# Rounded matmuls that walk their 512 columns as 64 lines of 8, in four passes

## The chip, the cores and the metric

The kernel runs on one core of one Trainium2 chip. The metric is the device time of one execution in microseconds (us), as the median of a few runs. Most executions of one kernel agree within 0.3%.

## The reference

The reference is an attention over a set, then a two-layer network. For each of four batches of 12,480 tokens with 128 features, 32 inducing vectors attend to the tokens, which gives 32 vectors `h`; then every token attends to these 32 vectors. The result, 49,920 tokens of 128 features, goes through the network.

```python
def mab(q, kv):
    s = scale * (q @ kv.transpose(0, 2, 1))
    s = s - s.max(-1, keepdims=True)
    a = np.exp(s)
    a /= a.sum(-1, keepdims=True) + 1e-09
    return a @ kv
h = mab(I, x)
x = mab(x, h)                       # 49,920 x 128
h = x @ w_in                        # 128 x 2048
g = h * (1.0 / (1.0 + np.exp(-1.702 * h)))
out = g @ w_out                     # 2048 x 128
```

## The kernel before

The tokens go through the network in blocks of 512, four blocks to a group of 2,048. A batch has six such groups (`s` = 0 to 5) and a rest of 192 tokens (`s` = 6); the rests of two batches together make one block of 384. The 2,048 hidden features are cut into 16 chunks of 128, and two chunks (`NG` = 8 pairs for a block) are one step `i` of the main loop (L1516).

The attention's weights are never multiplied with `h` by themselves. The kernel forms `hw` = `h` times `w_in` once for a batch, so that the hidden layer of a block is one product of `hw` with the block's attention weights. Both are stored in 32-row parts for the rounded value and what was left over by rounding, stacked to 128 rows: `st` (512 columns, of dtype `F32R`, a 4-byte float rounded for TensorE) is the stack of a block, `left` is that of a block of rests.

- `hidden` (L1368) issues for each of the two chunks one matmul: `hw` is the stationary operand (128x128), `st` the moving one (512 columns), and the output is half of a PSUM tile `ph` of two banks. For a block of rests it issues two of 192 columns for a chunk.
- `first` (L1382) calls `hidden`, and lets ScalarE apply the activation to `ph` (1,024 columns in one instruction) into `g`. Then ScalarE or VectorE writes `hi`, which is `g` rounded to `F32R`, and VectorE writes `lo` = `g` - `hi`.
- `second` (L1397) adds one chunk to the output: three matmuls with 128x128 weights, `hi` with the low part `wl` of `w_out`, `lo` with its high part `wh`, and `hi` with `wh`. All 48 of a block accumulate in one PSUM bank, `pso`. After the last, ScalarE copies the bank to `ob`, and a DMA stores it.

The first eight steps (`WHOLE` = 8) are done otherwise: `hidden` is the same, but their second layer is a product in plain float32 (`pso<-g,whole`), one matmul for a chunk.

The order of all engines' instructions is written out by a planner at build time. It keeps a clock for each engine, and costs (L277 for TensorE) that depend on the number of elements of an operand (`width`, L238) and on its dtype. `Clocks.names` (L87) tells which 512-column parts of some tiles an operand touches, from its first and last element. Beside the main loop run the attentions of the next batches, put between its steps. Their matmuls have 32 output rows (`128*32` in the profile) and run four side by side, one on each quarter of the array's columns.

Some of these walk their moving operand in lines already: `first_products` (L487) of batch 0, for the groups `s` whose tokens are not loaded a second time in rows (0, 3, 4 and 5: the list `LOADS` has `n6`, `n2` and `n1` alone), takes 16 lines of 32 columns, each fourth line of `xt`. Groups 2 and 1 take 512 columns in a row. By the order of `LOADS`, the groups' products come in the order 4, 3, 0, 5, 5 again (`TWICE`), 2, 1. `more_weights` (L1186) does the same with 12 of the 16 lines. The output of every matmul of this kernel is written to columns that lie side by side.

```python
xg = xg.rearrange("c (k g i) -> c g k i", g=g, i=32)      # first_products, batch 0
for j in range(g):
    pe_.matmul(pa[32 * j:32 * j + 32, 0:w], indT_sb, xg[:, j], start=True, stop=True)
```

Of the kernel before, what the change touches and what calls it, by code (L numbers as in the profile page):

```python
# [20 lines left out]
P = 128  # L21
# [42 lines left out]
S2 = ((6, 0), (1, 2, 3), (4, 5))  # L64
S2_LATER = ((0, 6), (1, 2, 3), (4, 5))
FB = 6
WINDOW = 100.0
CHAIN = 200.0
CALM = 0
# [4 lines left out]
class Clocks:  # L74
# [12 lines left out]
    def names(self, ap):  # L87
        name = ap.tensor.name
        if name not in self.halved:
            return [name]  # L90
        per = max(1, ap.ap[0][0] // (WC * len(self.halved[name])))
        at = ap.offset % ap.ap[0][0]
        end = (at + sum(step * (n - 1) for step, n in ap.ap[1:])) // per
        at //= per
        return self.halved[name][at // WC:end // WC + 1]
# [103 lines left out]
class Jobs:  # L199
# [13 lines left out]
    def step(self, limit=None, but=None):  # L213
        able = []
        for job in self.threads:
            eng, tiles, when = job[1]
            if eng is but or when is not None and not when():
                continue
            t = max(eng.t, self.clocks.ready(*(tiles() if callable(tiles) else tiles)))
            if limit is None or t <= limit(eng):  # L220
                able.append((t, job))
        if not able:
            return False
        soonest, job = min(able, key=lambda x: x[0])
        eng = job[1][0]
        t, job = min(
            [x for x in able if x[1][1][0] is eng and x[0] <= soonest + (CHAIN if x[1][2] <= -20 else WINDOW)],
            key=lambda x: (x[1][2], x[0]),
        )
        if self.idle:  # L230
            self.idle(t)
        job[1] = next(job[0], None)
        if job[1] is None:
            self.threads.remove(job)
        return True


def width(ap):  # L238
# [4 lines left out]
def set_attention_then_moe(ctx: ExitStack, tc, xT, x, indT, w_in, w_out, outT):  # L243
# [50 lines left out]
    pe_ = Meter(clocks, nc.tensor, tensor_cost, 220)  # L294
# [66 lines left out]
    hw = {}  # L361
# [514 lines left out]
    def start(pf, pw):  # L876
# [11 lines left out]
        for what in LOADS.split():  # L888
# [5 lines left out]
            elif what[0] == "n":  # L894
                if s < NS - 1:
                    t = pf.tile([P, BLK, P], F32, tag="xf", name="xf", bufs=FB)
                else:
# [114 lines left out]
        def turning(s, k0):  # L1012

            yield pe_, [xts[0, s]], bank("ph")
            if k0 == 0:
                turned[s] = pf.tile([P, BLK, P], F32, tag="xf", name="xf", bufs=FB)
            src = xts[0, s].rearrange("c (k t) -> c k t", t=P)
# [326 lines left out]
    def undivided(i):  # L1344

        yield pe_, lambda: [stacks[0, 0, 0], hw[0, i // 2]], bank(
            "ph", ("stack", 0), ("hw", i // 2), ("first", i - 1), ("second", i - AHEAD)
        )
        ph = hidden(i)
        hold("ph")  # L1350
        done.add(("first", i))
        yield act, [ph], has("exps")
        g = ph_.tile([P, 2, TOK], F32, tag="hi", name="g")
        act.activation(g, ph, AF.Gelu_apprx_sigmoid)
        hold("ph", -1)
        parts[i] = g, g
        done.add(("g", i))

    def undivided_seconds():

        while under_way:
            i, c = under_way[0]
            what = ("w_out", (2 * i + c) // 4)
            yield pe_, lambda: [parts[i][0], whole[(2 * i + c) // 4]], has(("g", i), what, *[("ahead", s) for s in AHEAD_S])
            second(*under_way.pop(0))
            done.add(("second", i))

    def hidden(i):  # L1368
        bi, k = divmod(i, NG)
        key, of = work[bi]  # L1370
        st = stacks[key]
        ph = ps_h.tile([P, 2, 512], F32, tag="ph", name="ph")
        for c in range(2):
            ch = 2 * k + c
            for b, at, w, _ in of:
                pe_.matmul(
                    ph[:, c, at:at + w], hw[b, ch // 4][:, ch % 4 * P:(ch % 4 + 1) * P],
                    st[:, at:at + w], start=True, stop=True,
                )
        return ph  # L1380

    def first(i):  # L1382
        ph = hidden(i)
        n = sum(p[2] for p in work[i // NG][1])
        hi = ph_.tile([P, 2, TOK], F32R, tag="hi", name="hi")
        lo = ph_.tile([P, 2, TOK], F32R, tag="lo", name="lo")
        g = pg.tile([P, 2, TOK], F32, tag="g", name="g")
        ph, hi, lo, g = ph[:, :, 0:n], hi[:, :, 0:n], lo[:, :, 0:n], g[:, :, 0:n]
        act.activation(g, ph, AF.Gelu_apprx_sigmoid)
        if act.t + 165 + 1.667 * n <= max(dve.t, act.t) + 150 + 1.06 * n:  # L1390
            act.activation(hi, ph, AF.Gelu_apprx_sigmoid)
        else:
            dve.tensor_copy(hi, g)
        dve.tensor_sub(lo, g, hi.bitcast(F32))
        parts[i] = hi, lo

    def second(i, c):  # L1397
        bi, k = divmod(i, NG)
        key, of = work[bi]
        n = sum(p[2] for p in of)  # L1400
        ch = 2 * k + c
        if ch == 0:
            outs[bi] = ps_o.tile([P, 512], F32, tag=f"po{bi % 2}", name="pso")
        o = outs[bi][:, 0:n]
        hi, lo = parts.pop(i) if c else parts[i]
        last = ch == NCH - 1
        if i < WHOLE:
            pe_.matmul(
                o, whole[ch // 4][:, ch % 4 * P:(ch % 4 + 1) * P], hi[:, c, :],
                start=(ch == 0), stop=last,  # L1410
            )
            if i >= WHOLE - NG and ch % 4 == 3:
                done.add(("whole", ch // 4))
        else:
            wlc, whc = [x[ch // 4][:, ch % 4] for x in (wl, wh)]
            pe_.matmul(o, wlc, hi[:, c, :], start=(ch == 0), stop=False)
            pe_.matmul(o, whc, lo[:, c, :], start=False, stop=False)
            pe_.matmul(o, whc, hi[:, c, :], start=False, stop=last)
        if last:
            ob = po.tile([P, TOK], F32, tag="ob", name="ob")  # L1420
            if bi == len(work) - 1:
                for k, (b, at, w, t0) in enumerate(of):
                    if k % 2:
                        dve.tensor_copy(ob[:, at:at + w], o[:, at:at + w])
                        nc.scalar.dma_start(outT[:, t0:t0 + w], ob[:, at:at + w])
                    else:
                        act.copy(ob[:, at:at + w], o[:, at:at + w])
                        sp.dma_start(outT[:, t0:t0 + w], ob[:, at:at + w])
                return
            act.copy(ob[:, 0:n], o)  # L1430
            for b, at, w, t0 in of:
                stores.append((i + 3, outT[:, t0:t0 + w], ob[:, at:at + w]))
            outs.pop(bi)
# [38 lines left out]
    n = len(work) * NG  # L1472
# [42 lines left out]
    i = WHOLE  # L1515
    while i < n or under_way:  # L1516
# [3 lines left out]
        if not begin_group(i):  # L1520
            at, c = under_way.pop(0)
            while not decoded(at, c):
                jobs.step(but=pe_)
            second(at, c)
        else:
            if back is None and turns and i >= begin[turns[0]] - LAST * (turns[0] not in es):
                back, laid = lay_out()
            while back is not None and first_block[laid] * NG <= i:
                late[0] = True
                run(back)  # L1530
                late[0] = False
                back = None
                if turns and first_block[turns[0]] * NG <= i:
                    back, laid = lay_out()
            bi, k = divmod(i, NG)
            while work[bi][0] not in stacks or any((p[0], k // 2) not in hw for p in work[bi][1]):
                jobs.step()
            while used["ph"] and jobs.step(but=pe_):
                pass
            while any(("two", q) not in done for q in range(min(G, (i + 4) // NG + 1))):  # L1540
                jobs.step(but=pe_)
            first(i)
            under_way += [(i, 0), (i, 1)]
            i += 1
            next(rest, None)
            if back is not None and next(back, 0) == 0:
                back = None
# [35 lines left out]
```

## Time and profile before

| | |
|---|---|
| median of 3 runs | 1539.06 us (1538.87 to 1539.07) |
| span of the profiled execution, first to last instruction | 1537.2 us (no time of its own is listed for it; the median of the runs is 1.9 us above its span) |
| TensorE matmul (PE) busy | 1529.9 us, 7736 instructions |
| TensorE weight load (PEld) busy | 1229.4 us |
| VectorE (DVE) busy | 1301.1 us |
| ScalarE (ACT) busy | 1345.4 us |
| mean granted TensorE clock | 1.000 |

Nearly every instruction has the line L181, because the planner's helper issues it; groups are told apart by their tiles. Matmuls are pipelined: each lasts longer than the distance between the starts of two neighbours, so the busy time of a group of matmuls is not their count times their duration. What a matmul costs the engine is the distance from its start to the next one's. The ends of matmuls are modelled.

### The profile page before, as it was taken

The page shows a single profiled execution, that of the slowest core. Times are in us where ns is not written, and L with a number is a line of the kernel's source. Part 1 is how long each engine was busy: PE and PEld are TensorE (multiplying, and loading weights), DVE is VectorE, ACT ScalarE, POOL GpSimd, SP SyncE. Part 2 cuts the span into 40 slices and gives each one's busy share as a digit, 9 for nine tenths or more (in the row PEclk, how much of TensorE's full clock was granted, in tenths as well). Part 3 has the DMA queues.
Part 4 walks back from the last instruction along what each step waited for, and adds up shares of the span by engine and source line. Part 5 has one row for each costly group of instructions (what it writes and reads, how often), then busy time and mean ns, then how long its engine had stood idle before and what let it go on. Part 6 is the DMA issues. An engine that isn't in the chain of part 4 may idle for free.

```text
span 1537.2 us, 21743 instructions
## 1 busy us (share of the span) xinstructions
PE 1529.9 (100%) x7736; PEld 1229.4 (80%) x7736; DVE 1301.1 (85%) x1512; ACT 1345.4 (88%) x1549; POOL 0.7 (0%) x6
## 2 busy tenths in 40 slices
PE   9999999999999999999999999999999999999999
PEld 6588878877888887877787887887788888888887
DVE  7988888789788887789789888778978888888886
ACT  4899989898999888889999888989899998888884
POOL 0000000000000000000000000000000000000000
PEclk9999999999999999999999999999999999999999
DMA  8210157713051115833133110872301101101100
GB/s 335 74 50 25 49 205 124 215 40 101 31 206 42 35 35 97 180 104 102 42 102 131 39 49 14 158 200 57 97 23 40 48 25 37 49 24 40 48 26 20
DMA packets 83849, 127.53 MB, mean 83 GB/s; under 512 B 12320, under 2 KB 50848, under 8 KB 77856
## 3 DMA queue, kind: packets, MB, share of 16 engines
q1 hardware_dynamic: 83600, 126.05, 28.8%
q8 instruction: 63, 1.03, 0.3%
q14 instruction: 42, 0.34, 0.1%
q10 hardware_dynamic: 144, 0.10, 0.0%
HBM read 72.11 MB, written 25.56 MB: 64 GB/s over the span
## 4 chain that ended last, share of the span: by engine, by line
PE 97%; DMA 1%; DVE 0%; ACT 0%; issue 0%; SPq 0%
PE pso L181 69%; PE ph L181 23%; PE pa L181 4%; DMA xt<-in_xT 1%; PE h L181 0%; ACT g L181 0%; PE spun L1268 0%; DMA hw<-tl 0%; DVE e L181 0%; DVE m L181 0%; DVE sm L181 0%; DVE two L181 0%; SPq L196 0%; DVE hw L181 0%; DVE w_in_all L181 0%
## 5 line engine op out<-in xcount | busy, mean ns | idle before, releaser
L181 DVE TENSOR_TENSOR lo<-g,hi 128x1024 fp32r<-128x1024 f32 x776 | 938.0, 1216 | 136.1 <-ACT hi L181 121.8
L181 ACT ACTIVATE g<-ph 128x1024 f32<-128x1024 f32 (+1 forms) x784 | 812.8, 1042 | 153.8 <-PE ph L181 74.7
L181 PE MATMUL pso<-hi,wl 128*128 128x512 f32 (+1 forms) x1552 | 603.7, 389 | 0.0
L181 PE MATMUL pso<-lo,wh 128*128 128x512 f32 (+1 forms) x1552 | 602.4, 388 | 0.0
L181 PE MATMUL pso<-hi,wh 128*128 128x512 f32 (+1 forms) x1552 | 602.3, 388 | 0.0
L181 ACT ACTIVATE hi<-ph 128x1024 fp32r<-128x1024 f32 (+1 forms) x493 | 512.6, 1040 | 0.0
L181 PE MATMUL ph<-st,hw 128*128 128x512 f32 x1536 | 474.9, 393 | 1.1 <-ACT g L181 1.1
L181 PEld LDWEIGHTS ph<-st,hw 128*128 128x128 f32 x1536 | 285.8, 188 | 77.0 <-issue 9.1
L181 PEld LDWEIGHTS pso<-hi,wl 128*128 128x128 f32 x1552 | 291.4, 188 | 62.8 <-issue 2.5
L181 PEld LDWEIGHTS pso<-hi,wh 128*128 128x128 f32 x1552 | 291.2, 188 | 59.6
L181 PEld LDWEIGHTS pso<-lo,wh 128*128 128x128 f32 x1552 | 291.4, 188 | 59.1
L181 DVE CAST hi<-g 128x1024 fp32r<-128x1024 f32 (+1 forms) x283 | 193.5, 684 | 73.8 <-ACT g L181 73.4
L181 ACT COPY ob<-pso 128x512 f32<-128x512 f32 (+1 forms) x98 | 60.0, 612 | 11.1 <-PE pso L181 11.1
L181 ACT ACT_TABLE_LOAD x26 | 33.4, 1283 | 1.2 <-PEq L1573 0.7
L181 PE MATMUL pa<-xt,indT_sb 128*32 128x512 f32 x200 | 24.9, 599 | 0.5 <-DMA xt<-in_xT 0.4
L181 ACT ACTIVATE s<-s,nmx 128x512 f32<-128x512 f32 (+1 forms) x27 | 17.8, 662 | 4.1 <-DVE nmx L181 4.0
L181 PE MATMUL pa<-xt,hT 128*32 128x512 f32 (+1 forms) x176 | 21.3, 593 | 0.0
L181 DVE TENSOR_TENSOR e<-e,sm 128x512 f32<-128x512 f32 (+3 forms) x29 | 17.8, 612 | 1.0
L181 DVE TENSOR_REDUCE m<-e 128x16 f32<-128x512 f32 (+2 forms) x28 | 17.3, 619 | 1.0
L181 DVE STREAM_TRANSPOSE aT<-s 128x512 f32<-128x512 f32 (+1 forms) x28 | 17.8, 640 | 0.2
L181 DVE TENSOR_REDUCE sm<-e 128x16 f32<-128x512 f32 (+3 forms) x29 | 17.3, 596 | 0.4 <-ACT e L181 0.4
L181 DVE TENSOR_TENSOR e<-e,m 128x512 f32<-128x512 f32 (+2 forms) x28 | 17.3, 617 | 0.0
(120 smaller groups left out, 356.9 us busy)
## 6 DMA issues: line engine op xcount, KB each, us to landing
xt<-in_xT SPq DMA_DIRECT2D x44, 1024.0 KB, 7.6
out_T<-ob SPq DMA_DIRECT2D x96, 256.0 KB, 2.0
xn<-in_x SPq DMA_DIRECT2D x72, 256.0 KB, 7.1
st<-ahT SPq DMA_DIRECT2D x184, 64.0 KB, 2.0
st<-alT SPq DMA_DIRECT2D x184, 64.0 KB, 2.0
raw<-in_w_in SPq DMA_DIRECT2D x4, 512.0 KB, 10.8
xf<-in_x SPq DMA_DIRECT2D x2, 1024.0 KB, 17.4
raw<-in_w_out SPq DMA_DIRECT2D x4, 512.0 KB, 15.3
```

The costliest lines, as they stand in the source:

```text
L181: return f(*a, **k)
```

## The change

A helper `strided` views an operand of 128 rows and *n* columns as four interleaved sets of lines: a line has 8 columns (32 bytes), and set *s* has the lines *s*, *s* + 4, *s* + 8 and so on. The engine walks set 0, then set 1, 2 and 3. For 512 columns a set has 16 lines, for 384 it has 12, for 192 it has 6. Both the moving operand and the output of a matmul get the same view, so that each column of the result is what it was and lies where it lay; only the order in which the columns pass is another. It is applied to the matmuls of `hidden` and to the three of `second` that work on `hi` and `lo`, not to the plain float32 products, to those of the attentions or to the weights.

```diff
+LINES = (4, 8)
...
+def strided(ap):
+
+    return ap.rearrange("p (n s i) -> p s n i", s=LINES[0], i=LINES[1])
...
                 pe_.matmul(
-                    ph[:, c, at:at + w], hw[b, ch // 4][:, ch % 4 * P:(ch % 4 + 1) * P],
-                    st[:, at:at + w], start=True, stop=True,
+                    strided(ph[:, c, at:at + w]), hw[b, ch // 4][:, ch % 4 * P:(ch % 4 + 1) * P],
+                    strided(st[:, at:at + w]), start=True, stop=True,
                 )
...
             wlc, whc = [x[ch // 4][:, ch % 4] for x in (wl, wh)]
-            pe_.matmul(o, wlc, hi[:, c, :], start=(ch == 0), stop=False)
-            pe_.matmul(o, whc, lo[:, c, :], start=False, stop=False)
-            pe_.matmul(o, whc, hi[:, c, :], start=False, stop=last)
+            by_lines, high, low = strided(o), strided(hi[:, c, :]), strided(lo[:, c, :])
+            pe_.matmul(by_lines, wlc, high, start=(ch == 0), stop=False)
+            pe_.matmul(by_lines, whc, low, start=False, stop=False)
+            pe_.matmul(by_lines, whc, high, start=False, stop=last)
```

## Rows read from the trace of the kernel before

**Rows 1.** The page's chain that ended last: shares by engine, then by line.

```profile
PE 97%; DMA 1%; DVE 0%; ACT 0%; issue 0%; SPq 0%
PE pso L181 69%; PE ph L181 23%; PE pa L181 4%; DMA xt<-in_xT 1%; PE h L181 0%; ACT g L181 0%; PE spun L1268 0%; DMA hw<-tl 0%; DVE e L181 0%; DVE m L181 0%; DVE sm L181 0%; DVE two L181 0%; SPq L196 0%; DVE hw L181 0%; DVE w_in_all L181 0%
```

**Rows 2.** Busy time (instructions) by stretch: PE, PEld, DVE, ACT, POOL; granted clock, DMA.

```profile
60.00:1500.00 1440.00, 1440.00 (x7040) 1162.82 (x7039) 1230.54 (x1378) 1290.80 (x1467) 0.00 (x0) 1.00 0.28 79
```

**Rows 3.** Whom TensorE waited for, whole span: us in total, times, longest.

```profile
PE spun L1268 <- POOL ident masks.py:199: 1.4, 1, 1.4
PE ph L181 <- ACT g L181: 1.1, 4, 0.5
```

**Rows 4.** Matmul groups by shape: busy us, mean ns of one, idle before.

```profile
L181 PE MATMUL pso<-hi,wl 128*128 128x512 f32 x1520 | 592.9, 390 | 0.0
L181 PE MATMUL pso<-lo,wh 128*128 128x512 f32 x1520 | 591.7, 389 | 0.0
L181 PE MATMUL pso<-hi,wh 128*128 128x512 f32 x1520 | 591.6, 389 | 0.0
L181 PE MATMUL ph<-st,hw 128*128 128x512 f32 x1536 | 474.9, 393 | 1.1 <-ACT g L181 1.1
...
L181 PE MATMUL pso<-hi,wl 128*128 128x384 f32 x32 | 10.8, 338 | 0.0
...
L181 PE MATMUL ph<-left,hw 128*128 128x192 f32 x64 | 9.4, 269 | 0.0
```

**Rows 5.** PE in order of time, mid-kernel: start us, us, instruction, merged count.

```profile
699.82 0.39 PE L181 MATMUL pso<-hi,wl 128*128 128x512 f32 x1
700.04 0.39 PE L181 MATMUL pso<-lo,wh 128*128 128x512 f32 x1
700.27 0.39 PE L181 MATMUL pso<-hi,wh 128*128 128x512 f32 x1
...
701.18 0.61 PE L181 MATMUL ph<-st,hw 128*128 128x512 f32 x2
701.63 0.39 PE L181 MATMUL pso<-hi,wl 128*128 128x512 f32 x1
...
703.44 0.39 PE L181 MATMUL pso<-hi,wh 128*128 128x512 f32 x1
```

**Rows 6.** The same view, the last block, of 384 columns.

```profile
1519.80 0.59 PE L181 MATMUL ph<-left,hw 128*128 128x192 f32 x4
1520.22 0.41 PE L181 MATMUL pso<-hi,wl 128*128 128x512 f32 x1
...
1526.32 0.33 PE L181 MATMUL pso<-hi,wl 128*128 128x384 f32 x1
...
1533.26 0.33 PE L181 MATMUL pso<-lo,wh 128*128 128x384 f32 x1
```

**Rows 7.** The same view: products of groups 0 and 5 (lines), and 1.

```profile
14.71 1.06 PE L181 MATMUL pa<-xt,indT_sb 128*32 128x512 f32 x8
15.71 1.97 PE L181 MATMUL ph<-ident,xt 128*128 128x128 f32 x16
17.70 1.07 PE L181 MATMUL pa<-xt,indT_sb 128*32 128x512 f32 x8
18.70 0.55 PE L181 MATMUL ph<-ident,xt 128*128 128x128 f32 x3
...
25.29 1.07 PE L181 MATMUL pa<-xt,indT_sb 128*32 128x512 f32 x8
26.28 0.49 PE L1268 MATMUL spun<-ident 128*128 128x128 f32 x2
```

**Rows 8.** The same view: 12 lines of 32 columns, then 512 columns.

```profile
38.39 0.83 PE L181 MATMUL pa<-xt,hT 128*32 128x384 f32 x8
...
39.03 1.04 PE L181 MATMUL pa<-xt,hT 128*32 128x512 f32 x8
39.89 0.25 PE L181 MATMUL h<-xt_last,hT 128*32 128x96 f32 x2
```

## The prediction

> **What bounds the kernel now.** I read the chain of waits first. It is TensorE in 97% of the span; the reader is to see that two tiles carry nearly all of it, `pso` with 69% and `ph` with 23%, and that both are written only by matmuls that the change touches, but for the few plain float32 ones [rows 1]. Then the busy time by stretch: from 60 to 1500 us TensorE is busy for all of the 1440 us, while VectorE has 1230.5 and ScalarE 1290.8 [rows 2]. The list of waits says the same from the other side: the two longest entries of TensorE come to 1.4 and 1.1 us [rows 3]. So there is no slack on TensorE. Whatever a rounded matmul gains or loses reaches the end in full, and a term that hides behind another engine does not exist here.
>
> [...] Next I took the distance between starts. From 699.82 to 703.44 us there are 16 matmuls of 512 columns (14 into `pso`, 2 into `ph`), 3.62 us, so 226 ns for one [rows 5]. In the last block 40 matmuls of 384 columns start between 1526.32 and 1533.26, 173.5 ns for one [rows 6]. [...] Matmuls that overwrite (`ph`) and that accumulate (`pso`) have the same distance [rows 5]. [...]
>
> **The change part by part.** No instruction is added, removed or moved. The planner's cost of a matmul goes by the product of its dimensions, still 512, and the first and last element of each operand stay, so the parts named stay too; the written-out order, the DMAs of SP and the waits should be those of before. The changed ones are 3 x 1520 + 1536 = 6096 matmuls of 512 columns, 3 x 32 = 96 of 384 and 64 of 192 [rows 4]. What changes inside each are three things.
>
> *Reading the moving operand in lines.* The trace has a near row. The products of groups 0 and 5 walk 16 lines of 32 columns, each fourth line; eight matmuls, in two sets of four side by side, take 15.71 - 14.71 = 1.00 and 18.70 - 17.70 = 1.00 us. Those of group 1, with 512 columns in a row, take 26.28 - 25.29 = 0.99 [rows 7]. With 12 lines the eight take 39.03 - 38.39 = 0.64, against 39.89 - 39.03 = 0.86 for 512 in a row [rows 8], and 0.86 x 384 / 512 = 0.645. So 2 x 15 jumps cost at most 0.01 us, 0.33 ns for a jump, and the second pair says -0.005 us for 2 x 11. I take 0. [...] These are plain float32 products with lines four times as long, hence "near", not "same".
>
> *Writing the output in lines.* No matmul of before writes columns that are not side by side, so no row shows it. [...] I take 0: a line is 8 whole columns, the same number of elements go out in the same number of clocks, and the row nearest to it, the reading in lines, shows nothing. This is the least certain step.
>
> [...]
>
> *The consumers.* ScalarE reads `ph` after both of its matmuls have ended, and the copy of `pso` comes after the 48th; the order of columns inside a matmul is over by then. 0.
>
> Sum: 0 on a span of 1537.2 us, to which 1.9 us come to reach the median 1539.06. Forecast 1539.1 us, with a range of its own of 1537.5 to 1541. [...]
>
> **The rivals.**
>
> [...]
>
> [...]
>
> [...]
>
> [...]
>
> E. *The view is flattened on its way into the instruction*, or the columns are taken in another order than written: 1539.1 us, not to be told from the forecast by time.
>
> **How the numbers follow.** Forecast and E together 0.60. A 0.14, B 0.07, C 0.07, in all 0.28 slower. D 0.12, spread evenly from 1459 to 1536. The range goes from 1500, which takes in half of D, to 1705, which takes in A with its rounding: 0.60 + 0.14 + 0.06 = 0.80. The upper bound of the read term, +128 us, lies inside it. C and B are left out. Faster by over 0.2%: 0.12; within: 0.60; slower: 0.28.
>
> **What would show it.** [...] If the distances are different for `ph` and `pso`, the accumulation is what cares about the order. TensorE should stay busy for 1440 of 1440 us, and the idle time of ScalarE and VectorE should grow only with the matmuls. The prediction is wrong if the distance moves by more than one nanosecond, or if it stays and a wait of TensorE on another engine appears.

## The result: 1559.9 us, 1.4% slower

The changed kernel takes 1559.92 us (median of 4 runs, 1559.64 to 1560.26), the kernel before 1539.0 us (4 runs, 1538.87 to 1539.07). The ratio is 1.0136, 95% interval 1.0122 to 1.0150. The profiled execution took 1560.26 us with a span of 1558.5 us, 21.3 us above the span of before.

The chain of the changed kernel's profile has the shares of [rows 1]; only the line numbers moved.

```profile
PE 97%; DMA 1%; DVE 0%; ACT 0%; issue 0%; SPq 0%
PE pso L182 69%; PE ph L182 23%; PE pa L182 4%; DMA xt<-in_xT 1%; PE h L182 0%; ACT g L182 0%; PE spun L1274 0%; DMA hw<-tl 0%; DVE e L182 0%; DVE m L182 0%; DVE sm L182 0%; DVE two L182 0%; SPq L197 0%; DVE hw L182 0%; DVE w_in_all L182 0%
```

The next row is its stretch from 60 to 1500 us, with the columns of [rows 2], and below it its two longest waits of TensorE, which answer to [rows 3].

```profile
60.00:1500.00 1440.00, 1440.00 (x6948) 1149.91 (x6947) 1213.01 (x1355) 1274.36 (x1448) 0.00 (x0) 1.00 0.28 78
```

```profile
PE spun L1274 <- POOL ident masks.py:199: 1.4, 1, 1.4
PE ph L182 <- ACT g L182: 1.1, 4, 0.5
```

TensorE is busy for the whole stretch as before, at the same granted clock, and waits for the same 1.4 and 1.1 us. It just got less done: 6948 matmuls where it was 7040. VectorE and ScalarE were busy for 17.5 and 16.4 us less in it, because less work reached them: 1355 instructions where it was 1378, and 1448 where it was 1467. So no wait was added; the distance from each rounded matmul to the next became longer. Mid-kernel, in order of time, answering to [rows 5]:

```profile
709.20 0.39 PE L182 MATMUL pso<-hi,wl 128*128 128x512 f32 x1
...
709.89 0.63 PE L182 MATMUL ph<-st,hw 128*128 128x512 f32 x2
710.36 0.39 PE L182 MATMUL pso<-hi,wl 128*128 128x512 f32 x1
...
712.89 0.39 PE L182 MATMUL pso<-hi,wl 128*128 128x512 f32 x1
```

Sixteen matmuls now start within 712.89 - 709.20 = 3.69 us, 230.6 ns each, where it was 3.62 us. Over all 512-column matmuls whose next start follows within 245 ns, the mean distance rose from 226.95 to 230.48 ns, for `ph` and for each of the three products of `pso` alike (230.4 to 230.6). 3.53 ns times 6096 matmuls is 21.5 us, against 21.3 us between the spans: that is the whole difference. Before, nearly every distance was 226 or 227 ns; now they repeat in fives, about 230, 230, 237, 228, 229.

The last block, with 384 columns, did not get slower. Between the two starts lie 40 distances, as in [rows 6]:

```profile
1547.85 0.34 PE L182 MATMUL pso<-lo,wh 128*128 128x384 f32 x1
...
1554.72 0.34 PE L182 MATMUL pso<-hi,wh 128*128 128x384 f32 x1
```

6.87 us for 40 is 171.8 ns, against 173.5. The same walk that costs 3.5 ns for 512 columns gives back 1.7 for 384. No price for each line or each pass can do that by itself.

### The profile page after: what moved, and what is told of

It is laid out like the page before. It is cut to its first block, busy times and chain, and to the rows that moved or that the text cites. A ratio compares the mean times of both kernels' runs of the same rounds, so it can differ in the third digit from the quotient of the medians.

```text
span 1558.5 us, 21743 instructions
## 1 busy us (share of the span) xinstructions
PE 1552.2 (100%) x7736; PEld 1235.1 (79%) x7736; DVE 1302.2 (84%) x1512; ACT 1347.1 (86%) x1549; POOL 0.7 (0%) x6
## 2 busy tenths in 40 slices
DMA packets 83849, 127.53 MB, mean 82 GB/s; under 512 B 12320, under 2 KB 50848, under 8 KB 77856
## 4 chain that ended last, share of the span: by engine, by line
PE 97%; DMA 1%; DVE 0%; ACT 0%; issue 0%; SPq 0%
PE pso L182 69%; PE ph L182 23%; PE pa L182 4%; DMA xt<-in_xT 1%; PE h L182 0%; ACT g L182 0%; PE spun L1274 0%; DMA hw<-tl 0%; DVE e L182 0%; DVE m L182 0%; DVE sm L182 0%; DVE two L182 0%; SPq L197 0%; DVE hw L182 0%; DVE w_in_all L182 0%
## 5 line engine op out<-in xcount | busy, mean ns | idle before, releaser
L182 PE MATMUL ph<-st,hw 128*128 128x512 f32 x1536 | 479.9, 397 | 1.1 <-ACT g L182 1.1
L182 PE MATMUL pa<-xt,hT 128*32 128x512 f32 (+1 forms) x176 | 21.3, 593 | 0.0
```

What stands on the lines that cost most here:

```text
L182: return f(*a, **k)
```

## The experiments

All kernels but the last were run once with a profile, beside a run of the kernel before on the same chip, which took between 1538.97 and 1539.27 us. The measure is the distance between starts. From 1200 to 1500 us the kernel before issues nothing on TensorE but the changed matmuls of 512 columns, so the length of that stretch divided by the number of matmuls in it is the distance. In the rows below, the columns are the stretch, its length, PE's busy time (matmuls), the granted clock and the DMA's share and rate. The kernel before, and the changed one:

```profile
1200.00:1500.00 300.00, 300.00 (x1324) 1.00 0.13 37
```

```profile
1200.00:1500.00 300.00, 300.00 (x1302) 1.00 0.12 36
```

300 / 1324 = 226.6 ns, 300 / 1302 = 230.4 ns.

### Which side pays: reading or writing

The two edits are against the changed kernel. First kernel: only the moving operand in lines.

```diff
-                    strided(ph[:, c, at:at + w]), ...
+                    ph[:, c, at:at + w], ...
...
-            by_lines, high, low = strided(o), strided(hi[:, c, :]), strided(lo[:, c, :])
+            by_lines, high, low = o, strided(hi[:, c, :]), strided(lo[:, c, :])
```

> Only the moving operand is walked in lines, the output is written in a row; the columns of the result therefore lie in another order than the reference's. Theory R (the reading of lines costs the 3.5 ns that the distance between starts grew, 226.95 to 230.5): 230.5 ns, 1560 us. Theory W (the writing of lines costs it): 227 ns, 1539 us. Theory B (each side a share): between, about 1550 us. The read rows before the change (lines of 32) speak for W.

Second kernel: only the output in lines.

```diff
-                    strided(st[:, at:at + w]), start=True, stop=True,
+                    st[:, at:at + w], start=True, stop=True,
...
-            by_lines, high, low = strided(o), strided(hi[:, c, :]), strided(lo[:, c, :])
+            by_lines, high, low = strided(o), hi[:, c, :], lo[:, c, :]
```

> Only the output is walked in lines, the moving operand is read in a row; the columns of the result lie in another order than the reference's. R: 227 ns, 1539 us. W: 230.5 ns, 1560 us. B: about 1550 us.

Measured: 1559.87 us for reading in lines, 1539.15 us for writing in lines. The two rows, in that order:

```profile
1200.00:1500.00 300.00, 300.00 (x1302) 1.00 0.12 36
```

```profile
1200.00:1500.00 300.00, 300.00 (x1324) 1.00 0.12 37
```

They are the counts of the changed kernel and of the kernel before, to the last matmul. Theory R holds, and W and B fall: with lines of 8, the whole cost is on the side that I had priced at 0 from a row (1559.87 against 1538.97 us), and the side that I called the least certain costs nothing that these runs tell (1539.15 against 1538.97 us).

### Other lengths of a line

`LINES = (4, 16)` and `LINES = (4, 4)`, everything else as in the changed kernel. In these and in all later kernels with lines, columns are read and written in lines together, so the two sides are parted for lines of 8 alone.

> Lines of 16 columns, still four sets: 32 lines and 4 passes for 512 columns. [...] Theory M (an operand of three steps costs, however it walks): 1560 us.

> Lines of 4 columns, four sets: 128 lines and 4 passes. [...]

Measured: 1615.12 us with lines of 16, 1533.01 us with lines of 4.

```profile
1200.00:1500.00 300.00, 300.00 (x1255) 1.00 0.12 36
```

```profile
1200.00:1500.00 300.00, 300.00 (x1332) 1.00 0.13 37
```

239.0 and 225.2 ns (over the whole kernel with lines of 4 the mean distance is 226.1, against 226.95 before). Fewer lines made it slower, more lines made it faster, and lines of 4 are even a little faster than columns in a row. M falls: three walks of three steps take 225.2, 230.4 and 239.0 ns. A price for each line falls too, since 32 lines take longer than 128, and so does a price for each pass, since all three have four. So columns in a row, 226.95 ns, are no floor for a matmul.

### Do the weights meet the moving operand?

While one matmul runs, the weights of the next are loaded; in the kernel before, the two start together, and the load lasts 0.19 us:

```profile
699.82 0.39 PE L181 MATMUL pso<-hi,wl 128*128 128x512 f32 x1
699.82 0.19 PEld L181 LDWEIGHTS pso<-lo,wh 128*128 128x128 f32 x1
```

Two kernels are made from the kernel before, with all columns in a row, to change the weights. One takes 96 of the 128 columns of the weights for the `lo` product, which then also writes 96 of the 128 rows of the output:

```diff
-            pe_.matmul(o, whc, lo[:, c, :], start=False, stop=False)
+            pe_.matmul(o[0:96], whc[:, 0:96], lo[:, c, :], start=False, stop=False)
```

> The kernel before the change (all walks in a row), but the product of lo takes 96 of the 128 columns of its weights and writes 96 of the 128 rows of the result; what is left out is a quarter of the lo term. [...] Theory A (a constant of the array at each change of weights): 226.7 ns everywhere, 1539 us.

The other changes only how the weights of all rounded products are read, at a step of two columns:

```diff
+def stepped(of, ch):
+
+    at = ch % 4 // 2 * 2 * P
+    return of[:, at + ch % 2:at + 2 * P:2]
...
-                    ph[:, c, at:at + w], hw[b, ch // 4][:, ch % 4 * P:(ch % 4 + 1) * P],
+                    ph[:, c, at:at + w], stepped(hw[b, ch // 4], ch),
...
-            wlc, whc = [x[ch // 4][:, ch % 4] for x in (wl, wh)]
+            wlc, whc = [stepped(x[ch // 4].rearrange("p c d -> p (c d)"), ch) for x in (wl, wh)]
```

> The kernel before the change, with all moving operands and outputs in a row, but the rounded products' weights are read with a step of two columns over 256, so that a product mixes the weights of two chunks and the result is another. [...] A: 226.7 ns, 1539 us.

Measured: 1562.78 and 1577.49 us; the rows in that order, the second with the first and last of 40 starts in its last block.

```profile
1200.00:1500.00 300.00, 300.00 (x1303) 1.00 0.12 36
```

```profile
1200.00:1500.00 300.00, 300.00 (x1287) 1.00 0.12 36
```

```profile
1565.05 0.34 PE L181 MATMUL pso<-lo,wh 128*128 128x384 f32 x1
...
1571.99 0.33 PE L181 MATMUL pso<-hi,wh 128*128 128x384 f32 x1
```

230.2 and 233.1 ns; for 384 columns and stepped weights 6.94 / 40 = 173.5 ns, as before the change. Theory A falls: nothing about the moving operand or the output of the second kernel differs from the kernel before, the weights alone are read in another order, and the distance at 512 columns becomes 6.5 ns longer. With fewer weights the distances became longer too, and uneven (229 to 233 ns by product, where A said 226.7 everywhere). In that first kernel the shorter load (0.16 us where it was 0.19) and the fewer rows written are not parted. The second shows that the order of the weights has a price; that this price depends on how the columns are read, the sections below show. Here the order of the weights alone moved the time by 38 us.

### What in the walk decides

The lengths above also changed the distance from one line of a set to the next, and other numbers of sets separate the two: `LINES = (8, 4)`, `(16, 4)`, `(2, 8)`, `(2, 4)`.

> The change with eight sets of lines of 4 columns (8 passes, 128 lines): the next line of a set begins 32 columns on, as with the change itself, while lines are as short as in the run with lines of 4. Theory S (the distance from line to line decides: 16 columns gave 226.1 ns, 32 gave 230.5, 64 gave 239.5): 230.5 ns, 1560 us. Theory N (the length of a line decides: 4 columns gave 226.1, 8 gave 230.5, 16 gave 239.5): 226.1 ns, 1533 us.

> Sixteen sets of lines of 4 columns: the next line of a set begins 64 columns on, as with lines of 16 in four sets. S: 239.5 ns, 1615 us. N: 226.1 ns, 1533 us.

> The change with two sets instead of four: lines of 8 columns as before, 64 of them, but the next line of a set begins 16 columns on and there are two passes. Theory S and N as they stand have both failed. [...] Theory N (length of a line): 230.5 ns, 1560 us.

> Two sets of lines of 4 columns: 128 lines, the next line of a set begins 8 columns on. [...] N: 226.1 ns, 1533 us.

Measured: 1658.35, 1844.47, 1574.14 and 1574.24 us, in that order. The rows, in the same order (with sixteen sets the stretch is later, since that kernel's last attention products lie beyond 1200 us):

```profile
1200.00:1500.00 300.00, 300.00 (x1218) 1.00 0.11 34
```

```profile
1500.00:1800.00 300.00, 300.00 (x1088) 1.00 0.10 30
```

```profile
1200.00:1500.00 300.00, 300.00 (x1288) 1.00 0.12 36
```

```profile
1200.00:1500.00 300.00, 300.00 (x1287) 1.00 0.12 36
```

246.3, 275.7, 232.9 and 233.1 ns. S and N fall. A single kernel then ran nineteen treatments of five blocks each:

```diff
+WALKS = [(1, 1, 1), (4, 8, 1), (4, 4, 1), (2, 2, 1), ...]     # sets, columns of a line, step of the weights
...
+def walk(bi):
+
+    return WALKS[max(0, bi - 1) // 5 % len(WALKS)]
```

> One kernel, nineteen treatments of five blocks each, in the order: a row; then sets x columns of a line 4x8 (the change), 4x4, 2x2, 4x2, 8x2, 2x16, 2x32, 2x64, 2x128, 4x32, 4x64, 8x8, 8x16, 8x32, 32x4; then a row with weights read at a step of four columns; 4x4 with weights at a step of two; 16x2. Where weights are read at a step, a product mixes weights of several chunks, so its result is another. Read is the distance between starts within a treatment. [...] Theory G (the number of sets decides, at least for 2, 8 and 16, which gave 232.8, 246.5 and 278): all walks of 2 sets 232.8, of 8 sets 246.5, 16x2 278, 32x4 over 300. Theory K (the memory that the moving operand and the weights are read from is divided by address, and lines that lie a multiple of 64 columns apart fall on the same part): 2x32, 2x64, 2x128, 4x32, 4x64, 8x8, 8x16, 8x32, 32x4 all at 239 ns or more, those nearer together less. Theory C (the weight load clashes with the moving read): the two treatments with stepped weights differ from the same walk without, a row at step four from 227, 4x4 at step two from 226. If weights and moving read do not meet, both stay.

The whole kernel took 1841.26 us. These are stretches inside treatments (sets x columns of a line), with nothing else on TensorE: a row, 4x8, 2x2, 4x2, 8x2, 2x16, 2x32, 2x64, 2x128, 4x32, 4x64, 32x4, a row with weights at step four, 4x4 with weights at step two, 16x2. A count includes one or two matmuls that only touch an edge.

```profile
73.68:126.98 53.30, 53.30 (x237) 1.00 0.19 65
146.45:180.12 33.67, 33.67 (x147) 1.00 0.19 55
348.87:408.79 59.92, 59.92 (x135) 1.00 0.22 62
464.78:531.21 66.43, 66.43 (x146) 1.00 0.05 15
597.92:725.05 127.13, 127.13 (x302) 1.00 0.06 17
732.60:783.00 50.40, 50.40 (x211) 1.00 0.12 34
836.27:857.67 21.40, 21.40 (x94) 1.00 0.86 196
895.75:925.14 29.39, 29.39 (x131) 1.00 0.28 81
972.60:1012.72 40.12, 40.12 (x178) 1.00 0.29 96
1051.16:1118.13 66.97, 66.97 (x289) 1.00 0.15 43
1126.20:1158.62 32.42, 32.42 (x145) 1.00 0.06 21
1441.28:1519.19 77.91, 77.91 (x293) 1.00 0.10 30
1527.38:1594.54 67.16, 67.16 (x287) 1.00 0.11 32
1602.56:1640.00 37.44, 37.44 (x169) 1.00 0.15 43
1677.30:1808.17 130.87, 130.87 (x302) 1.00 0.06 17
```

By the starts within the treatments: a row 226.8 and 4x8 230.6 ns, as in kernels of their own; 2x16 240, 2x32 236.7 (the stretch above alone gives at most 21.40 / 92 = 232.6), 4x32 233.3, 32x4 266.8; 2x64 227.0 and 2x128 226.7, no cost. The three walks of eight sets with longer lines lie near 233 ns (8x8 233, 8x16 232, 8x32 236, medians). G falls (two sets go from 226.7 to 240 ns, eight with lines of 4 and more from 232 to 246), and K falls too (4x64 gave 226.7 and 2x128 no more, though their lines lie 256 columns apart). Lines of 2 columns stand by themselves: 452 ns (2x2, the median), 461 (4x2), 431 (8x2, median) and 440 (16x2, median), about twice the time of a row. The reading and the writing were not parted there. With weights at step four, a row goes to 234.8 ns, while 4x4 goes from 226.1 (the kernel with lines of 4) to 223.8 with weights at step two. Stepped weights thus cost beside columns in a row and gain beside lines of 4.

### The best pair as a whole kernel

Lines of 4 and weights at step two can be had with the right result: a chunk becomes every second one of 256 hidden features, and `w_out` is laid out with neighbouring chunks' columns in turn. The edit is against the changed kernel; the rounded products, and the first block's plain ones, read their weights through `stepped`.

```diff
-LINES = (4, 8)
+LINES = (4, 4)
...
+def stepped(of, ch):
+
+    at = ch % 4 // 2 * 2 * P
+    return of[:, at + ch % 2:at + 2 * P:2]
...
-            w_out.reshape(-1, P, w_out.shape[1]).transpose(1, 0, 2).reshape(P, -1)
+            w_out.reshape(-1, P, 2, w_out.shape[1]).transpose(1, 0, 3, 2).reshape(P, -1)
```

> A whole kernel with the best pair that the treatments showed: moving operand and output in four sets of lines of 4 columns, and the weights of the rounded products (and of the first block's plain ones) read at a step of two columns. The result is the reference's: a chunk now is every second of 256 hidden features, and w_out is laid out beforehand so that each chunk's columns alternate with its neighbour's. Theory C (weight load and moving read meet in the memory, and the two orders together set the distance): 223.9 ns as in the treatment, against 226.1 with lines of 4 alone and 226.95 before; 6096 x 3.1 = 19 us less than before, 1520 us. If the treatment's value was owed to something else than the orders (the place in the kernel, the mixed weights' data), 226.1 ns as in the run with lines of 4, 1533 us.

Measured: 1521.17 us (4 runs, 1521.09 to 1521.67), against 1539.1 us for the kernel before (7 runs). The ratio is 0.9883, 95% interval 0.9866 to 0.9899: 1.2% faster than the kernel before, and close to what theory C expected.

```profile
1200.00:1500.00 300.00, 300.00 (x1348) 1.00 0.12 36
```

300 / 1348 = 222.6 ns; 16 of these matmuls have 192 columns, since this kernel is further on by then. The mean over its 512-column matmuls is 223.9, as in the treatment. 3.1 ns less on each of 6096 is 18.9 us, close to the gain of 17.9 us.

With this kernel there are four that differ in the two orders. Their mean distances over the whole kernel are, with columns in a row, 226.95 ns (weights in a row) and 233.3 (weights at step two), and with lines of 4, the output too, 226.1 and 223.9. The step of the weights costs 6.3 ns in the first pair and gains 2.2 in the second. If each order had a price of its own, the step would have changed both pairs by the same amount; so the two orders act on each other. That much of theory C is shown; that they meet in the memory is not.

The weight loads' own times speak for it too. These are the loads for the `lo` product (us in total, mean ns of one, idle us before them) in the kernel before, with eight sets of lines of 4, with stepped weights, and in the last kernel:

```profile
L181 PEld LDWEIGHTS pso<-lo,wh 128*128 128x128 f32 x1552 | 291.4, 188 | 59.1
L182 PEld LDWEIGHTS pso<-lo,wh 128*128 128x128 f32 x1552 | 298.8, 193 | 81.2
L181 PEld LDWEIGHTS pso<-lo,wh 128*128 128x128 f32 x1552 | 299.8, 193 | 60.5
L182 PEld LDWEIGHTS pso<-lo,wh 128*128 128x128 f32 x1552 | 304.1, 196 | 41.9
```

The second kernel reads its weights as the first does; only the walk of the columns, read and written, is another, and the load became 193 ns instead of 188. A longer load does not by itself make a longer distance: the last kernel has the longest loads of the four and the shortest distance.

## Why the range held and the likeliest case did not

The time lies within the stated range, 1500 to 1705 us; the forecast itself, no change, was wrong by its own sign, a distance that moves by more than one nanosecond. That the range held is luck. No run shows the prices of the written walk from which 1459, 1500 and 1705 us come; in their place the runs showed 3.5 ns on each matmul of 512 columns, and nothing of it on the written side (1539.15 against 1538.97 us).

- *What bounds the kernel*: right. TensorE stayed busy for 1440 of 1440 us, the waits stayed, and 3.53 ns on each of 6096 matmuls reached the end in full (21.5 us by that product, 21.3 us of span).
- *No instruction, wait or DMA changes*: borne out as far as the profile shows it, 21,743 instructions and 83,849 DMA packets in both.
- *Reading the moving operand in lines, "I take 0"*: this is the step that failed. The reading costs all of it, 20.9 us. Two things were wrong with the near row of [rows 7, 8]. It could not show a cost this small: 3.5 ns over 63 jumps is 0.056 ns each, and the row told no less than 0.33. And it was a row of plain float32 products with 32 columns of weights, not of rounded ones with 128: rounded matmuls with lines of the same 32 columns, 128 columns apart, took 233.3 ns instead of 226.8 (4x32, the output walked too). Which of these differences matters was not tested. The bound from that row, 0.33 ns for each of 63 jumps on 6096 matmuls, 128 us, held.
- *Writing the output in lines, 0*: right, 0.2 us between single runs, though I called it the least certain.
- *The same distance for `ph` and `pso`*, 226 ns [rows 5]: right, and so after the change, 230.4 to 230.6 ns. But all matmuls that were compared, of two widths and two kinds, had the same two orders of reading. Changing either order moves the distance at 512 columns: 6.3 ns up with stepped weights, 0.9 ns down with lines of 4, 3.1 down with both (means over the whole kernels). A faster kernel, to which I gave 0.12, was possible (1521.17 us with both), only not with this walk.
- *384 columns*, 173.5 ns before: 171.8 ns now, less, where 512 columns went from 226.95 to 230.48. A price for each jump or each return to the front would have made both longer.

What stays open is the rule. Shown are that with lines of 8 the reading side pays, that the weights' order alone changes the distance, that the two orders act on each other, and that no single one of line length, distance between lines, number of lines or number of sets decides (4x4 226.1 ns, 8x4 246.3 and 2x4 233.1 with the same length and number of lines; 4x8 230.4 with the distance of 8x4; 2x16 240 and 2x64 227.0 with the same number of sets). Why the orders act on each other is not shown; K, the one cause that was put to the test, fell. Why the distances repeat, in fives with lines of 8 and in fours with lines of 4 (about 218, 230, 224, 221), is not explained, nor why 384 columns take another price than 512.

## What to carry to other kernels

A price that is the same in all rows of a trace may be a constant, or all rows may share the thing that sets it; before it is written off, change that thing once: 226 ns in every row became 223.9 to 233.3 when an order of reading changed. A row of another kind of instruction bounds a cost at best, and no finer than its digits, here 0.33 ns for a jump where 0.056 counted; it does not set it to zero. And where a matmul's operands can be laid out freely, the order in which both are read is worth a sweep (1521.17 against 1539.1 us here): one kernel with a treatment for each group of blocks showed nineteen in one run.

## What was not expected of the hardware

- With lines of 2 columns a rounded matmul of 512 columns takes 431 to 461 ns instead of 227, whereas four sets of lines of 4 take 226.
- Loading 96 instead of 128 columns of weights in a quarter of the matmuls, which then write 96 rows, made the kernel slower, 1562.78 against 1539.27 us.
- The order of the weights costs or gains by the order of the columns: a step of two is 6.3 ns slower beside columns in a row and 2.2 ns faster beside lines of 4.
- The same order of reading can cost at one width and gain at another: 4x8 is 3.5 ns slower at 512 columns and 1.7 ns faster at 384.
